# Layer scale, x + gamma * y: loads in one order on the SP queue, stores held back on the ACT queue, pieces of 40, 37, 40 and 11 rows

## The chip, the cores and the metric

The kernel runs on one core of a Trainium2 chip. The metric is the device time of one execution in microseconds (us). Beside it stands a profile of one execution, whose span runs from the first to the last instruction of the core. Engines are named as in the profile: PE is TensorE, DVE is VectorE, ACT is ScalarE, POOL is GpSimd, SP is SyncE; ACTq and SPq are the queues from which ACT and SP issue DMAs.

## The reference

```python
B, S, D = 1024, 16, 512          # x, y: [B, S, D] bfloat16, gamma: [D] bfloat16

def reference(x, y, gamma):
    return x + gamma * y
```

x, y and the output have 16.78 MB each, so 33.56 MB are read and 16.78 MB are written.

## The kernel before

The 16384 rows of 512 elements (1 KB each) are split over the 128 partitions, so that each partition owns 128 consecutive rows, 128 KB of each tensor. The kernel cuts these 128 rows into four pieces of 32 (`PIECE`, line 5). Every DMA moves one piece of one tensor: 4 MB, as 128 packets of 32 KB, one for each partition. The 16 DMA engines serve eight partitions each.

All of y has room on the core (`y_sb`, 128 KB per partition), and the result is written over it. x has two buffers of 32 rows (`xs`, line 46), so the third piece of x can be loaded only when the first has been added, and the fourth when the second has.

At the start a small DMA brings gamma, PE copies it to all partitions by a matrix product with a row of ones, and DVE writes that to `gamma_sb`. Then DVE works through the pieces in order (lines 95 to 113): it waits for y's piece, multiplies it by gamma in place (line 98), waits for x's piece, and adds x (line 104).

The order of the transfers is written out by hand, for two queues:

- ACT issues gamma, then the four loads of y one behind the other, then waits for the second piece's add and stores piece 1, waits for the fourth add and stores piece 3 (lines 86 to 93).
- SP issues x pieces 0 and 1, waits for the first add, issues x piece 2, waits for the second add, issues x piece 3 and the store of piece 0, waits for the third add and stores piece 2 (lines 75 to 83).

So loads of x and y run side by side on two queues, and stores begin behind loads on both. The first loads are moved to the front of the program (lines 118 to 124). `_take` (line 9) waits for a semaphore and subtracts what it waited for. SP waits at the end for both queues' stores (lines 115 and 116).

Of the kernel before, what the change touches and what calls it, by code (L numbers as in the profile page):

```python
# [3 lines left out]

PIECE = 32
MULT, ADD = mybir.AluOpType.mult, mybir.AluOpType.add


def _take(sem, n, eng):


    return eng.wait_ge(sem, n).then_inc(sem, -n)  # L12


def kernel(
    tc: tile.TileContext,
    x: bass.AP,
    y: bass.AP,
    gamma: bass.AP,
    out: bass.AP,  # L20
):

    nc = tc.nc
    P = nc.NUM_PARTITIONS
    tc.close()
    tc.compile()  # L29

    xf = x.flatten_outer_dims()
    yf = y.flatten_outer_dims()
    of = out.flatten_outer_dims()
    N, D = xf.shape
    rows = N // P
    n = rows // PIECE
    dt = xf.dtype
    xv = xf.rearrange("(p n) d -> p n d", p=P)
    yv = yf.rearrange("(p n) d -> p n d", p=P)
    ov = of.rearrange("(p n) d -> p n d", p=P)  # L40

    gamma_row = nc.alloc_sbuf_tensor("gamma_row", [1, D], dt).ap()
    ones_row = nc.alloc_sbuf_tensor("ones_row", [1, P], dt).ap()
    gamma_sb = nc.alloc_sbuf_tensor("gamma_sb", [P, D], dt).ap()
    y_sb = nc.alloc_sbuf_tensor("y_sb", [P, rows, D], dt).ap()
    xs = [nc.alloc_sbuf_tensor(f"x{i}", [P, PIECE, D], dt).ap() for i in range(2)]
    gamma_ps = nc.alloc_psum_tensor("gamma_ps", [P, D], mybir.dt.float32).ap()

    sem = nc.alloc_semaphore
    s_gamma, s_ones, s_ps, s_dve = sem("s_gamma"), sem("s_ones"), sem("s_ps"), sem("s_dve")  # L50
    s_x = [sem(f"s_x{c}") for c in range(n)]
    s_y = [sem(f"s_y{c}") for c in range(n)]
    s_sp, s_act = sem("s_sp"), sem("s_act")
    s_out_sp, s_out_act = sem("s_out_sp"), sem("s_out_act")

    def piece(c):
        return slice(c * PIECE, (c + 1) * PIECE)

    first = []

    def load(eng, dst, src, s):
        return eng.dma_start(out=dst, in_=src).then_inc(s, 16)


    first.append(load(nc.scalar, gamma_row, gamma.unsqueeze(0), s_gamma))
    nc.vector.memset(ones_row, 1.0).then_inc(s_ones, 1)  # L66
    _take(s_ones, 1, nc.tensor)
    _take(s_gamma, 16, nc.tensor)
    nc.tensor.matmul(gamma_ps, ones_row, gamma_row, start=True, stop=True).then_inc(s_ps, 1)  # L69
    _take(s_ps, 1, nc.vector)  # L70
    nc.vector.tensor_copy(out=gamma_sb, in_=gamma_ps).then_inc(s_dve, 1)  # L71
    _take(s_dve, 1, nc.vector)


    first.append(load(nc.sync, xs[0], xv[:, piece(0), :], s_x[0]))
    first.append(load(nc.sync, xs[1], xv[:, piece(1), :], s_x[1]))
    _take(s_sp, 1, nc.sync)
    load(nc.sync, xs[0], xv[:, piece(2), :], s_x[2])
    _take(s_sp, 1, nc.sync)
    load(nc.sync, xs[1], xv[:, piece(3), :], s_x[3])  # L80
    nc.sync.dma_start(out=ov[:, piece(0), :], in_=y_sb[:, piece(0), :]).then_inc(s_out_sp, 16)
    _take(s_sp, 1, nc.sync)
    nc.sync.dma_start(out=ov[:, piece(2), :], in_=y_sb[:, piece(2), :]).then_inc(s_out_sp, 16)


    for c in range(n):
        i = load(nc.scalar, y_sb[:, piece(c), :], yv[:, piece(c), :], s_y[c])
        if c < 2:
            first.append(i)
    _take(s_act, 1, nc.scalar)  # L90
    nc.scalar.dma_start(out=ov[:, piece(1), :], in_=y_sb[:, piece(1), :]).then_inc(s_out_act, 16)
    _take(s_act, 1, nc.scalar)
    nc.scalar.dma_start(out=ov[:, piece(3), :], in_=y_sb[:, piece(3), :]).then_inc(s_out_act, 16)

    for c in range(n):
        yt = y_sb[:, piece(c), :]
        _take(s_y[c], 16, nc.vector)
        nc.vector.tensor_tensor(  # L98
            out=yt, in0=yt, in1=gamma_sb[:, None, :].to_broadcast([P, PIECE, D]), op=MULT
        ).then_inc(s_dve, 1)  # L100
        _take(s_x[c], 16, nc.vector)
        _take(s_dve, 1, nc.vector)

        i = nc.vector.tensor_tensor(out=yt, in0=xs[c % 2], in1=yt, op=ADD)  # L104
        if c == 0:
            i.then_inc(s_sp, 1)
        elif c == 1:
            i.then_inc(s_dve, 1)
            _take(s_dve, 1, nc.vector)
            nc.vector.sem_inc(s_sp, 1)  # L110
            nc.vector.sem_inc(s_act, 1)
        else:
            i.then_inc(s_sp if c == 2 else s_act, 1)

    _take(s_out_sp, 32, nc.sync)
    _take(s_out_act, 32, nc.sync)

    main = nc.main_func.blocks[0].instructions
    names = {i.ins.name for i in first}
    for b in nc.main_func.blocks[1:]:  # L120
        for i in [i for i in b.instructions if i.name in names]:
            b.instructions.remove(i)
    for k, i in enumerate(first):
        main.insert(1 + k, i.ins)


# [1 line left out]
_INS = ['x', 'y', 'gamma']  # L128
_OUTS = [((1024, 16, 512), 'bfloat16')]


# [23 lines left out]
```

## Time and profile before

| what | value |
|---|---|
| time, median of 10 runs | 121.17 us (120.83 to 121.4) |
| the profiled execution's own time | 121.16 us |
| its span, first to last instruction | 119.8 us |
| DVE busy | 70.3 us (59%), four multiplies and four adds of 8.69 us |
| first multiply starts, last add starts | 24.38 us, 86.34 us |
| moved | 50.33 MB, mean 420 GB/s |
| the two DMA queues' packet time | 49.9% and 48.7% of 16 engines' span |

In the profile's slices each digit is the busy share of a fortieth of the span in tenths. A queue's share is the time of its packets divided by the time of 16 engines over the whole span. q1 is the SP queue, q10 the ACT queue. An operation of VectorE is told as output<-inputs, partitions x elements and type. "L104" is line 104 of the kernel; waits show line 12, the helper `_take`. The trace also holds a record for every DMA packet: its start, its duration, its size and its queue.

### The profile page before, as it was taken

What the parts mean: (1) busy time and instruction counts of PE and PEld (TensorE: products, weight loads), DVE (VectorE), ACT (ScalarE), POOL (GpSimd) and SP (SyncE); (2) the same over time, 40 slices, a digit from 0 to 9 for tenths busy, and PEclk for the clock granted to TensorE, in tenths of its full rate; (3) what the DMA queues carried; (4) which work ended last, traced back from release to release, by engine and by line L of the source; (5) the groups of instructions that cost most, each with busy time, mean ns of one, the idle gap of its engine ahead of it and who ended that gap; (6) DMA issues with size and microseconds to landing.
All of it is one profiled execution on the core that took longest, in us unless ns stands there. A gap on an engine that the chain in (4) does not pass through costs nothing. (4 is left out here: it accounts for less than half of the span.)

```text
span 119.8 us, 90 instructions
## 1 busy us (share of the span) xinstructions
PE 0.6 (0%) x1; PEld 0.1 (0%) x1; DVE 70.3 (59%) x10; POOL 0.2 (0%) x4
## 2 busy tenths in 40 slices
PE   0100000000000000000000000000000000000000
PEld 0000000000000000000000000000000000000000
DVE  0100000089999999999899999999999700000000
POOL 0000000000000000000000000000000000000000
DMA  8999998989898989999999999999999999999994
GB/s 252 448 394 481 394 481 372 503 350 525 350 514 361 503 372 481 394 470 405 427 448 394 481 394 394 394 394 470 405 459 416 448 427 438 427 427 448 405 459 197
DMA packets 1730, 50.33 MB, mean 420 GB/s; under 512 B 193, under 2 KB 194, under 8 KB 194
## 3 DMA queue, kind: packets, MB, share of 16 engines
q1 hardware_dynamic: 864, 25.17, 49.9%
q10 hardware_dynamic: 866, 25.17, 48.7%
HBM read 33.56 MB, written 16.78 MB: 420 GB/s over the span
## 5 line engine op out<-in xcount | busy, mean ns | idle before, releaser
L98 DVE TENSOR_TENSOR y_sb<-y_sb,gamma_sb 128x16384 bf16<-128x16384 bf16 x4 | 34.8, 8690 | 18.9 <-DVEq L12 18.9
L104 DVE TENSOR_TENSOR y_sb<-x,y_sb 128x16384 bf16<-128x16384 bf16 x4 | 34.8, 8692 | 0.6
L71 DVE CAST gamma_sb<-gamma_ps 128x512 bf16<-128x512 f32 x1 | 0.7, 692 | 2.6 <-DVEq L12 2.6
L66 DVE MEMSET ones_row<- 1x128 bf16 x1 | 0.2, 165 | 2.7 <-PEq L29 2.7
L69 PE MATMUL gamma_ps<-gamma_row,ones_row 1*128 1x512 bf16 x1 | 0.6, 581 | 4.7 <-PEq L12 4.7
L69 PEld LDWEIGHTS gamma_ps<-gamma_row,ones_row 1*128 1x128 bf16 x1 | 0.1, 98 | 4.7 <-issue 4.7
L139 POOL MEMSET const-bfloat16-1.0<- 128x1 bf16 x1 | 0.1, 101 | 0.0
L139 POOL MEMSET const-uint8-127<- 128x1 uint8 x1 | 0.1, 101 | 0.0
L139 POOL MEMSET const-float32-0.0<- 128x1 f32 x1 | 0.1, 98 | 0.2 <-issue 0.2
L139 POOL MEMSET const-float32-1.0<- 128x1 f32 x1 | 0.1, 98 | 0.0
## 6 DMA issues: line engine op xcount, KB each, us to landing
x<-in_x_dram SPq DMA_DIRECT2D x4, 4096.0 KB, 24.7
y_sb<-in_y_dram ACTq DMA_DIRECT2D x4, 4096.0 KB, 47.3
out_dram<-y_sb ACTq DMA_DIRECT2D x2, 4096.0 KB, 30.5
out_dram<-y_sb SPq DMA_DIRECT2D x2, 4096.0 KB, 41.9
gamma_row<-in_gamma_dram ACTq DMA_DIRECT2D x1, 1.0 KB
```

The lines of the kernel that those rows point to most:

```text
L66: nc.vector.memset(ones_row, 1.0).then_inc(s_ones, 1)
L69: nc.tensor.matmul(gamma_ps, ones_row, gamma_row, start=True, stop=True).then_inc(s_ps, 1)
L71: nc.vector.tensor_copy(out=gamma_sb, in_=gamma_ps).then_inc(s_dve, 1)
L98: nc.vector.tensor_tensor(out=yt, in0=yt, in1=gamma_sb[:, None, :].to_broadcast([P, PIECE, D]), op=MULT).then_inc(s_dve, 1)
L104: i = nc.vector.tensor_tensor(out=yt, in0=xs[c % 2], in1=yt, op=ADD)
L139: nc = _bacc.Bacc("TRN2", target_bir_lowering=False, num_devices=1)
```

## The change

Every load is issued by SP, in one list: x and y piece 0 (40 rows), x and y piece 1 (37 rows), all the rest of y (51 rows in one DMA), x piece 2 (40 rows), x piece 3 (11 rows). The x buffer is one tensor of 77 rows; x piece 2 takes the place of piece 0, so its load waits for the first add, and x piece 3 lies within the place of piece 1, so its load waits for the second. Gamma stays with ACT, which otherwise issues only the stores, now two of 64 rows each (64 KB per partition). The first store waits for `s_go`, which PE sends once the load of x rows 77 to 117 has landed, and for the first two adds; the second waits for all four adds. DVE learns of that landing from PE too (`s_rel`). Adds count up one semaphore (`s_add`), and both stores count up one (`s_out`), which SP reads at the end. On DVE the order of operations is the same, on pieces of the new sizes.

```diff
--- before.py
+++ after.py
@@ -2,7 +2,20 @@
 import concourse.tile as tile
 from concourse import mybir
 
-PIECE = 32
+PIECES = [40, 37, 40, 11]
+SP = [('x', 0, 40, 0), ('y', 0, 40), ('x', 40, 77, 40), ('y', 40, 77), ('y', 77, 128), ('x', 77, 117, 0), ('x', 117, 128, 40)]
+ACT = [('g',), ('s', 0, 64), ('s', 64, 128)]
+EARLY = (2, 1)
+RELEASE = ('x', 77, 117, 0)
+DVE = [('m', 0), ('a', 0), ('m', 1), ('a', 1), ('m', 2), ('a', 2), ('m', 3), ('a', 3)]
 MULT, ADD = mybir.AluOpType.mult, mybir.AluOpType.add
 
 
@@ -22,7 +35,6 @@
 
 
 
     nc = tc.nc
     P = nc.NUM_PARTITIONS
     tc.close()
@@ -33,7 +45,9 @@
     of = out.flatten_outer_dims()
     N, D = xf.shape
     rows = N // P
-    n = rows // PIECE
+    n = len(PIECES)
+    assert sum(PIECES) == rows
+    starts = [sum(PIECES[:c]) for c in range(n + 1)]
     dt = xf.dtype
     xv = xf.rearrange("(p n) d -> p n d", p=P)
     yv = yf.rearrange("(p n) d -> p n d", p=P)
@@ -43,26 +57,70 @@
     ones_row = nc.alloc_sbuf_tensor("ones_row", [1, P], dt).ap()
     gamma_sb = nc.alloc_sbuf_tensor("gamma_sb", [P, D], dt).ap()
     y_sb = nc.alloc_sbuf_tensor("y_sb", [P, rows, D], dt).ap()
-    xs = [nc.alloc_sbuf_tensor(f"x{i}", [P, PIECE, D], dt).ap() for i in range(2)]
+    x_loads = [w for w in SP + ACT if w[0] == "x"]
+    y_loads = [w for w in SP + ACT if w[0] == "y"]
+    stores = [w for w in SP + ACT if w[0] == "s"]
+    for loads in (x_loads, y_loads, stores):
+        assert sum(w[2] - w[1] for w in loads) == rows
+    x_rows = max(w[3] + w[2] - w[1] for w in x_loads)
+    x_sb = nc.alloc_sbuf_tensor("x_sb", [P, x_rows, D], dt).ap()
     gamma_ps = nc.alloc_psum_tensor("gamma_ps", [P, D], mybir.dt.float32).ap()
 
     sem = nc.alloc_semaphore
     s_gamma, s_ones, s_ps, s_dve = sem("s_gamma"), sem("s_ones"), sem("s_ps"), sem("s_dve")
-    s_x = [sem(f"s_x{c}") for c in range(n)]
-    s_y = [sem(f"s_y{c}") for c in range(n)]
-    s_sp, s_act = sem("s_sp"), sem("s_act")
-    s_out_sp, s_out_act = sem("s_out_sp"), sem("s_out_act")
-    def piece(c):
-        return slice(c * PIECE, (c + 1) * PIECE)
-    first = []
-    def load(eng, dst, src, s):
-        return eng.dma_start(out=dst, in_=src).then_inc(s, 16)
-    first.append(load(nc.scalar, gamma_row, gamma.unsqueeze(0), s_gamma))
+    s_load = {w: sem("s_" + "_".join(map(str, w[:2]))) for w in x_loads + y_loads}
+    s_add, s_go, s_rel, s_end, s_out = sem("s_add"), sem("s_go"), sem("s_rel"), sem("s_end"), sem("s_out")
+    added = [a for kind, *a in DVE if kind == "a"]
+    order = {a[0]: k for k, a in enumerate(added)}
+    def meets(a, b, c, d):
+        return a < d and c < b
+    def pieces_of(a, b):
+        return [c for c in range(n) if meets(starts[c], starts[c + 1], a, b)]
+    def x_at(row):
+        return next(w[3] + row - w[1] for w in x_loads if w[1] <= row < w[2])
+    def frees(w):
+        old = x_loads[: x_loads.index(w)]
+        old = [v for v in old if meets(v[3], v[3] + v[2] - v[1], w[3], w[3] + w[2] - w[1])]
+        return [c for v in old for c in pieces_of(v[1], v[2])]
+    early = []
+    def ring(eng, what, n_early):
+        known, went = 0, False
+        for k, w in enumerate(what):
+            kind = w[0]
+            need = frees(w) if kind == "x" else pieces_of(w[1], w[2]) + list(w[3:]) if kind == "s" else []
+            need = max((order[c] + 1 for c in need), default=0)
+            if kind == "s" and not went:
+                _take(s_go, 1, eng)
+                went = True
+            if need > known:
+                eng.wait_ge(s_add, need)
+                known = need
+            if kind == "g":
+                i = eng.dma_start(out=gamma_row, in_=gamma.unsqueeze(0)).then_inc(s_gamma, 16)
+            elif kind == "x":
+                to = x_sb[:, w[3] : w[3] + w[2] - w[1], :]
+                i = eng.dma_start(out=to, in_=xv[:, w[1] : w[2], :]).then_inc(s_load[w], 16)
+            elif kind == "y":
+                r = slice(w[1], w[2])
+                i = eng.dma_start(out=y_sb[:, r, :], in_=yv[:, r, :]).then_inc(s_load[w], 16)
+            else:
+                r = slice(w[1], w[2])
+                i = eng.dma_start(out=ov[:, r, :], in_=y_sb[:, r, :]).then_inc(s_out, 16)
+            if k < n_early:
+                early.append(i.ins)
+    ring(nc.sync, SP, EARLY[0])
+    ring(nc.scalar, ACT, EARLY[1])
     nc.vector.memset(ones_row, 1.0).then_inc(s_ones, 1)
     _take(s_ones, 1, nc.tensor)
     _take(s_gamma, 16, nc.tensor)
@@ -71,57 +129,51 @@
     nc.vector.tensor_copy(out=gamma_sb, in_=gamma_ps).then_inc(s_dve, 1)
     _take(s_dve, 1, nc.vector)
 
-    first.append(load(nc.sync, xs[0], xv[:, piece(0), :], s_x[0]))
-    first.append(load(nc.sync, xs[1], xv[:, piece(1), :], s_x[1]))
-    _take(s_sp, 1, nc.sync)
-    load(nc.sync, xs[0], xv[:, piece(2), :], s_x[2])
-    _take(s_sp, 1, nc.sync)
-    load(nc.sync, xs[1], xv[:, piece(3), :], s_x[3])
-    nc.sync.dma_start(out=ov[:, piece(0), :], in_=y_sb[:, piece(0), :]).then_inc(s_out_sp, 16)
-    _take(s_sp, 1, nc.sync)
-    nc.sync.dma_start(out=ov[:, piece(2), :], in_=y_sb[:, piece(2), :]).then_inc(s_out_sp, 16)
-    for c in range(n):
-        i = load(nc.scalar, y_sb[:, piece(c), :], yv[:, piece(c), :], s_y[c])
-        if c < 2:
-            first.append(i)
-    _take(s_act, 1, nc.scalar)
-    nc.scalar.dma_start(out=ov[:, piece(1), :], in_=y_sb[:, piece(1), :]).then_inc(s_out_act, 16)
-    _take(s_act, 1, nc.scalar)
-    nc.scalar.dma_start(out=ov[:, piece(3), :], in_=y_sb[:, piece(3), :]).then_inc(s_out_act, 16)
-    for c in range(n):
-        yt = y_sb[:, piece(c), :]
-        _take(s_y[c], 16, nc.vector)
-        nc.vector.tensor_tensor(
-            out=yt, in0=yt, in1=gamma_sb[:, None, :].to_broadcast([P, PIECE, D]), op=MULT
-        ).then_inc(s_dve, 1)
-        _take(s_x[c], 16, nc.vector)
-        _take(s_dve, 1, nc.vector)
-        i = nc.vector.tensor_tensor(out=yt, in0=xs[c % 2], in1=yt, op=ADD)
-        if c == 0:
-            i.then_inc(s_sp, 1)
-        elif c == 1:
-            i.then_inc(s_dve, 1)
-            _take(s_dve, 1, nc.vector)
-            nc.vector.sem_inc(s_sp, 1)
-            nc.vector.sem_inc(s_act, 1)
+    _take(s_load[RELEASE], 16, nc.tensor)
+    nc.tensor.sem_inc(s_go, 1)
+    nc.tensor.sem_inc(s_rel, 1)
+    landed, open_mults = set(), 0
+    def need(loads, c):
+        for w in loads:
+            if w not in landed and meets(starts[c], starts[c + 1], w[1], w[2]):
+                if w == RELEASE:
+                    _take(s_rel, 1, nc.vector)
+                else:
+                    _take(s_load[w], 16, nc.vector)
+                landed.add(w)
+    for kind, *args in DVE:
+        c = args[0]
+        yt = y_sb[:, starts[c] : starts[c + 1], :]
+        if kind == "m":
+            need(y_loads, c)
+            g = gamma_sb[:, None, :].to_broadcast([P, PIECES[c], D])
+            nc.vector.tensor_tensor(out=yt, in0=yt, in1=g, op=MULT).then_inc(s_dve, 1)
+            open_mults += 1
         else:
-            i.then_inc(s_sp if c == 2 else s_act, 1)
-    _take(s_out_sp, 32, nc.sync)
-    _take(s_out_act, 32, nc.sync)
+            need(x_loads, c)
+            if open_mults:
+                _take(s_dve, open_mults, nc.vector)
+                open_mults = 0
+            at = x_at(starts[c])
+            xt = x_sb[:, at : at + PIECES[c], :]
+            nc.vector.tensor_tensor(out=yt, in0=xt, in1=yt, op=ADD).then_inc(s_add, 1)
+    nc.scalar.sem_inc(s_end, 1)
+    _take(s_end, 1, nc.sync)
+    _take(s_add, n, nc.sync)
+    _take(s_out, 16 * len(stores), nc.sync)
 
     main = nc.main_func.blocks[0].instructions
-    names = {i.ins.name for i in first}
+    names = {i.name for i in early}
     for b in nc.main_func.blocks[1:]:
         for i in [i for i in b.instructions if i.name in names]:
             b.instructions.remove(i)
-    for k, i in enumerate(first):
-        main.insert(1 + k, i.ins)
+    for k, i in enumerate(early):
+        main.insert(1 + k, i)
 
 
 # ---- launch: one core; inputs and outputs as the reference has them ----
```

## The prediction

> **What bounds the kernel now.** I read the busy shares, then the slices, the queues, the stretches, and last the timeline around the final store.
>
> ```profile
> span 119.8 us, 90 instructions
> PE 0.6 (0%) x1; PEld 0.1 (0%) x1; DVE 70.3 (59%) x10; POOL 0.2 (0%) x4
> ...
> DMA  8999998989898989999999999999999999999994
> ...
> DMA packets 1730, 50.33 MB, mean 420 GB/s; under 512 B 193, under 2 KB 194, under 8 KB 194
> ...
> q1 hardware_dynamic: 864, 25.17, 49.9%
> q10 hardware_dynamic: 866, 25.17, 48.7%
> ```
>
> The only busy compute engine works 59% of the span; the two DMA queues together hold the 16 engines for 98.6% of it, 118.1 us. 1730 less 194 small packets leaves 1536 large ones, 96 per engine of 32 KB each (one partition's rows of one piece), so 1.23 us a packet. In the trace's packet records the usual packet takes 1.213 us. The mean is higher for four reasons, per engine: the first packets (start 1.00 to 1.36 us into the span, mean 1.858) lose 0.64; the next two 0.03; packets between 44 and 73 us average 1.216 and lose 0.08; and around 73 to 77 us, where the first store meets the last x load, two load packets lose 0.79. Sum for the slowest engine: 1.36 + 96 x 1.213 + 1.54 + 12 semaphore packets of 0.009 = 119.4 us, and the last packet does end at 119.39. Landing adds 0.33, the end of the program 0.11: 119.83. The execution lasts 121.16, so 1.36 lies around the span; the median of the runs is 121.17, so the two can be compared directly.
>
> The stretches show the same rate with loads only and with stores only, and the dip between (columns: stretch, length, busy time of PE, PEld, DVE, POOL, clock, DMA share, GB/s):
>
> ```profile
> 5.00:72.00 67.00, 0.26 (x1) 0.00 (x0) 47.43 (x7) 0.00 (x0) 1.00 1.00 432
> 72.00:78.00 6.00, 0.00 (x0) 0.00 (x0) 5.83 (x2) 0.00 (x0) 1.00 1.07 404
> 78.00:118.00 40.00, 0.00 (x0) 0.00 (x0) 16.89 (x2) 0.00 (x0) 1.00 1.00 433
> ```
>
> The last rows of the timeline (start, length):
>
> ```profile
> 86.34 8.69 DVE L104 TENSOR_TENSOR y_sb<-x,y_sb 128x16384 bf16<-128x16384 bf16 x1
> 95.14 0.35 ACTq L93 DMA_DIRECT2D out_dram<-y_sb  x1
> ```
>
> VectorE ends at 95.03, the last store is issued 0.11 later, and 24 us of stores are still to drain. So the engines' bytes set the end, and VectorE only through when it releases a store.
>
> **What the Trainium skill says.** "DMA: Bandwidth & Descriptors", section "Where 436 GB/s comes from", gives a ceiling of 435.2 GB/s; the 432 and 433 above are 99% of it. Same page, "Issuing engines are not separate DMA queues": DMAs of any issuer share the 16 engines. The trace agrees: from 36 to 45 us only the ACT ring has packets, across the boundary from the second to the third y load, and they still follow each other every 1.21 us. So one ring for loads costs nothing by itself. Same page, "Latency and other measured facts": first byte on this path after about 0.6 us, memory latency 0.2 us, 2 us at high load. Here the first load's packet came 1.0 us after issue on idle engines; what load adds is the slow rival below.
>
> **The change, part by part.** *Bytes*: unchanged, 3 x 128 rows of 1 KB on each of 128 partitions; a row on all partitions is 8 KB per engine, 8/32 x 1.213 = 0.303 us.
>
> *Fewer, larger packets*: seven loads and two stores make 8 x 9 = 72 packets per engine, not 96. An 8 KB instruction-fetch packet takes 0.3075 us; four are 1.230 against 1.213, so a packet has a fixed part of 0.017/3 = 0.006 us. 24 fewer: -0.14, -0.03 with three fewer semaphore packets. Bounds: 0 (if a 64 KB row is cut in two or the fixed part belongs to fetches only, near 0) to -0.25.
>
> *Two rings to one for the loads*: the 0.08 lost between 44 and 73 us is with two rings, 36 to 44 us on one ring shows none. I take -0.08, bounds -0.08 to +0.1.
>
> *First store*: the 0.79 loss cannot vanish by order alone; a stream must turn from loads to stores once. Nearest row: the first load, 0.64. I take that, -0.15; bounds -0.79 to +0.5.
>
> *Waits*: I lay out the new order for the slowest engine (start 1.36 + 0.67 = 2.03, then 0.303 a row, landing 0.33). y0 ends after 80 rows and lands at 26.6 (24.3 before). VectorE needs 8.69/32 = 0.272 us a row and operation, 0.15 from multiply to add, -0.08 from add to multiply, as before; eight operations and 69.5 us in all either way. Piece 0 ends at 48.6. y1 (154 rows) lands at 49.05, half a microsecond of idle. Piece 1 ends at 69.4, piece 2 at 91.1 (y2 and x2 landed long before), piece 3 at 97.2. SP's wait for add 0 stands before x2, its wait for add 1 before x3; queued behind these waits are only those two loads. SP passes the second at 69.4, while x2 runs until 76.3, so x3 is in the ring 7 us early. PE's wait for x2 stands behind the finished matmul and holds up nothing; VectorE takes its word at about 80, where it is three microseconds old. The stores are queued behind ACT's wait for it: x2 lands at 76.65, and four semaphore steps of 0.11 give an issue at 77.1. Cover until its first packet: x3, 11 rows, until 2.03 + 256 x 0.303 = 79.65, 2.5 us. The first store (64 rows, 19.4 us) then ends at 79.65 + 0.64 + 19.4 = 99.65. The second needs add 3, 97.2: issued at 97.3, 2.3 us ahead. With the 1.0 to 1.4 us of the first load both leads suffice. If the second's cover is gone, each microsecond of delay beyond it is a microsecond of time.
>
> *Rest*: SP's final waits and ACT's handover to it come before the last landing and cost nothing under it; shared counting of the stores is read only at its full value. Gamma's path still ends 20 us before the first multiply.
>
> Sum: 121.16 - 0.14 - 0.03 - 0.08 - 0.15 = 120.76.
>
> **Rivals.** *A, continuous transfers*, as summed: 120.8, by itself 120.5 to 121.1. *B, the turn to stores costs nothing*: then the first store ends at 99.0, and VectorE's chain takes over: issue 97.3, packets from 98.7 on the slowest engine, start-up 0.64 if the ring is nearly dry, 19.4 of data, 0.44 to the end, 1.36 around: 120.5. For it: after the turn 40 us of stores run at full rate; against it: the one start and the one turn in this trace both paid.
>
> *C, stores start late and leave the engines dry; slower.* Under load the trace shows long delays from issue to first packet: third x load 3.4 to 4.6 us (issue 42.0), last store 4.1 to 4.8 (95.14). If that is latency and not queueing, the store issued at 77.1 starts around 77.1 + 3.8 = 80.9, 1.2 us after the loads end; the second then finds its ring hardly dry, since the first is late too. 120.8 + 1.2 = 122.0. It decides once the delay exceeds the leads of 2.5 and 2.3 us. For it: the delays themselves. Against it: each is about 1.0 us plus the packet in service and one or two more of the other ring, which looks like packets already taken in, and gamma's packet, issued at 0.13 to 0.65, came at 2.95 behind one single packet of x.
>
> *D, nothing gained*: packets cost by bytes alone, and the turn costs 0.79 again or a dry spell of some tenths stands ahead of the second store: 121.1.
>
> **How the numbers follow.** A 0.42, B 0.18, C 0.22, D 0.18. A measurement of this kernel can tell about 0.2%, 0.24 us, from no change: faster is below 120.93. Most of A (0.37) and B (0.18) give faster 0.55; D and the slow side of A give same 0.22; C, 0.22, and the end of D slower 0.23. Forecast 120.8, that of A. The range from 120.4 to 121.9 takes in A, B, D and the milder part of C, and leaves out about 0.18. A and B alone: 120.4 to 121.1.
>
> **What would show it.** Right: loads at 432 GB/s on one queue without a gap until 79 to 80 us; the first store issued at about 77.1; the last add ending at about 97.2 and the last store issued at once; no DMA slice under 9 at 79 or 99 us; span 119.4. The turn shows as slow packets at 79. C would show as a dip there or ahead of the second store; B as an end 21 to 22 us after VectorE's last add. Wrong altogether: load packets above 1.213 us per 32 KB, stores of 64 KB rows slower per byte, or an add ending after 99.

## The result, and the profile after

The changed kernel takes 120.00 us (median of 8 runs, 119.92 to 120.06), the kernel before 121.23 in the runs beside it: a ratio of 0.9898, 95% interval 0.9888 to 0.9909. That is 1.2 us gained where 0.4 was forecast, and 0.4 us below the low end of the range, 120.4.

The page of the changed kernel, first the shares and slices, then the queues:

```profile
span 118.8 us, 84 instructions
...
PE 0.6 (0%) x1; PEld 0.1 (0%) x1; DVE 70.2 (59%) x10; POOL 0.2 (0%) x4
...
DMA  7999999999999999979696999998899889988891
...
DMA packets 1299, 50.33 MB, mean 424 GB/s; under 512 B 146, under 2 KB 147, under 8 KB 147
...
q1 hardware_dynamic: 1008, 33.55, 66.0%
q10 hardware_dynamic: 290, 16.78, 32.6%
```

VectorE is as busy as before. The loads are 66.0% of the engines' span on SP's queue and the stores 32.6% on ACT's: 98.6% together, the same as before, of a span 1.0 us shorter. 1299 less 147 small packets leaves 1152 large ones, 72 per engine. The single digits of 6 and 7 in the middle of the slice row (50 to 65 us), and the 8s from 80 us on, are no dry spells: this view books a packet where it starts, and the packets are now long against a slice of 2.97 us (1.93 us for 51 rows, 2.42 for 64). In the packet records each engine's packets follow one another there without a pause. The stretches show the same distortion when they are short (stretch, length, busy times, clock, DMA share, GB/s):

```profile
75.00:79.00 4.00, 0.00 (x0) 0.00 (x0) 4.00 (x1) 0.00 (x0) 1.00 0.82 344
79.00:82.00 3.00, 0.00 (x0) 0.00 (x0) 2.85 (x2) 0.00 (x0) 1.00 1.62 700
```

344 and then 700 GB/s is a row of 64 KB store packets that all begin just after 79 us, not a pause and a burst. Where a fraction of a microsecond matters, the packet records have to be read instead, as below.

The timeline around the two stores (start, length; the ACTq row merges both stores, from the first issue to the end of the second):

```profile
69.41 10.82 DVE L153 TENSOR_TENSOR y_sb<-y_sb,gamma_sb 128x20480 bf16<-128x20480 bf16 x1
77.06 20.75 ACTq L116 DMA_DIRECT2D out_dram<-y_sb  x2
...
94.35 3.09 DVE L162 TENSOR_TENSOR y_sb<-x_sb,y_sb 128x5632 bf16<-128x5632 bf16 x1
```

The first store is issued at 77.06 and the last add ends at 97.44, against 77.1 and 97.2 in the forecast: the schedule came out as laid out. What differs is in the packets. I compare each packet with the usual (median) packet of its size (11 KB 0.422 us, 32 KB 1.213, 64 KB 2.418), and call what is over that the excess. It is summed over all packets and divided by the 16 engines. The turn is the time in which loads end and stores begin, 72 to 78 us before and 76 to 80 after.

| | before | after |
|---|---|---|
| all packets at their usual time | 116.45 | 116.24 |
| excess of the first packets | 0.64 | 0.66 |
| excess at the turn from loads to stores | 0.79 | 0.04 |
| other excess | 0.11 | 0.10 |
| last packet ends, us in the span | 119.39 | 118.33 |

So 0.75 of the 1.06 us by which the last packet ends earlier is the turn, and 0.21 is the fewer packets. Before, every engine has one to three load packets at the turn that take up to 2.3 us instead of 1.213. After, no packet there is more than 0.1 us over its usual time. The store packets that follow are not shorter than usual in either kernel, so the time is lost and not only moved. The experiments ask why.

### The profile page after: what moved, and what is told of

Same layout as the page of the kernel before. It is cut to its first block, busy times and chain, and to the rows that moved or that the text cites. A ratio compares the mean times of both kernels' runs of the same rounds, so it can differ in the third digit from the quotient of the medians.

```text
span 118.8 us, 84 instructions
## 1 busy us (share of the span) xinstructions
PE 0.6 (0%) x1; PEld 0.1 (0%) x1; DVE 70.2 (59%) x10; POOL 0.2 (0%) x4
## 2 busy tenths in 40 slices
DMA packets 1299, 50.33 MB, mean 424 GB/s; under 512 B 146, under 2 KB 147, under 8 KB 147
## 3 DMA queue, kind: packets, MB, share of 16 engines
q10 hardware_dynamic: 290, 16.78, 32.6%
## 5 line engine op out<-in xcount | busy, mean ns | idle before, releaser
L153 DVE TENSOR_TENSOR y_sb<-y_sb,gamma_sb 128x20480 bf16<-128x20480 bf16 (+2 forms) x4 | 34.8, 8688 | 20.7 <-DVEq L25 20.7
L162 DVE TENSOR_TENSOR y_sb<-x_sb,y_sb 128x20480 bf16<-128x20480 bf16 (+2 forms) x4 | 34.8, 8692 | 0.6
```

The source lines that it names most:

```text
L153: nc.vector.tensor_tensor(out=yt, in0=yt, in1=g, op=MULT).then_inc(s_dve, 1)
L162: nc.vector.tensor_tensor(out=yt, in0=xt, in1=yt, op=ADD).then_inc(s_add, 1)
```

## The experiments

The expectations name theories of what makes load packets slow at the turn:

- T1: the turn costs something only while load packets of the other queue are still to come.
- T2: it costs something only if a store is queued behind a load on its own queue.
- T3: it always costs the same, or the slow packets don't come from the turn at all.
- T4, after the first four runs: it costs whenever stores are known to the engines while loads are still to be served.
- T5, also after these: it depends on the queue that the stores use.

**The kernel before with its first ACT store held.** The idea was to move only the start of the store.

```diff
+    _take(s_y[3], 16, nc.tensor)
+    nc.tensor.sem_inc(s_go, 1)
+    nc.tensor.sem_inc(s_rel, 1)
...
+    _take(s_go, 1, nc.scalar)
     _take(s_act, 1, nc.scalar)
     nc.scalar.dma_start(out=ov[:, piece(1), :], in_=y_sb[:, piece(1), :]).then_inc(s_out_act, 16)
```

> Kernel before, with one edit: the first store of the ACT queue (piece 1) is issued only once the last y load has landed, so that its packets reach the engines when the x load on the other queue is nearly through. Theory T1 (a turn from loads to stores costs 0.8 us only while load packets of the other queue are still being served; after them it is free): the slow packets of 73 to 77 us are gone, 121.2 - 0.7 = 120.5 us, x piece 3 landing at about 80 instead of 85. T2 (the cost comes from a store queued behind a load on its own queue): the first store is no longer queued, also about 120.5. T3 (the slow stretch is not tied to the turn, or is a cost that any turn pays): 121.2, and the stretch is still there, at the new turn or at 73 us.

Measured 121.12 us, ratio 0.9994 (0.9982 to 1.0006): no gain. x landed at 80.1 to 80.6 as expected, but slow load packets stood at 77 us, 0.44 us per engine. Two stores could be the cause: SP's store of piece 0, which was still queued behind x piece 3 and which the expectation of T2 overlooked, and ACT's own, issued at 76.78 while packets of x were running until 80.2. So this run decides neither T1 nor T2.

**The first store on SP, unheld.**

```diff
-SP = [..., ('x', 117, 128, 40)]
-ACT = [('g',), ('s', 0, 64), ('s', 64, 128)]
+SP = [..., ('x', 117, 128, 40), ('s', 0, 64)]
+ACT = [('g',), ('s', 64, 128)]
```

> Changed kernel, with the first store moved from the ACT queue to the end of the SP queue, right behind the last x load, with no hold on it but the two adds. T1 (only mixing costs): loads and stores still follow each other, no slow packets, 120.0 us. T2 (a store queued behind a load costs): 0.6 to 0.8 us of slow packets at 79 us, about 120.7. T3: 120.0.

Measured 121.70 us, ratio to before 1.0035 (1.0023 to 1.0047), 1.7 us above the changed kernel. The store is issued at 69.77:

```profile
69.77 0.44 SPq L116 DMA_DIRECT2D out_dram<-y_sb  x1
```

The load packets of 77 to 80 us carry 0.83 us of excess although no store packet runs before 79.9: a store waiting behind them is enough. Loads and store share one queue here, so T1 is out. A second cost, not expected: the last store, first on the ACT queue when SP's runs out, begins with 0.79 us of excess per engine at 99 us.

**32-row pieces, early and late release.** Two kernels that differ only in how x piece 3 is loaded, and in which part releases the stores:

```diff
-SP = [..., ('x', 64, 96, 0), ('x', 96, 128, 32)]
-RELEASE = ('x', 64, 96, 0)
+SP = [..., ('x', 64, 96, 0), ('x', 96, 117, 32), ('x', 117, 128, 53)]
+RELEASE = ('x', 96, 117, 32)
```

> Changed kernel with four pieces of 32 rows and four stores of 32 rows, the stores released when x piece 2 has landed: 32 rows of x piece 3 are still to be loaded when the first store comes, so the two are mixed for some 15 us. T1: the slow packets are back at about 71 to 75 us, 0.8 us; with 16 more packets per engine (0.1) 120.9 us. T2: no store is queued behind a load, no slow packets, 120.1. T3: 120.1. The last add would end at about 96, some 13 us ahead of need, so no dry spell under any.

> As the kernel with four pieces of 32 rows, but x piece 3 is loaded as 21 and 11 rows, and the stores are released when the 21 rows have landed: only 11 rows are left when the first store comes, as in the changed kernel. T1: no slow packets, 0.8 us less than with the early release, 120.1 us. T2 and T3: same as with the early release, within 0.1.

Measured 121.09 us (early; ratio 0.9995, 0.9985 to 1.0005) and 120.13 us (late; 0.9912, 0.9892 to 0.9931). The rows of the stores in the timeline, merged from the first issue on, early release and then late:

```profile
70.73 26.79 ACTq L116 DMA_DIRECT2D out_dram<-y_sb  x4
```

```profile
77.24 19.88 ACTq L116 DMA_DIRECT2D out_dram<-y_sb  x4
```

The slow packets are in the first, 0.8 us of excess at 72 to 75, and at the turn of the second at most 0.01. The view of one stretch, early release and then late:

```profile
66.00:90.00 24.00, 0.00 (x0) 0.00 (x0) 22.34 (x4) 0.00 (x0) 1.00 1.02 425
```

```profile
66.00:90.00 24.00, 0.00 (x0) 0.00 (x0) 22.69 (x4) 0.00 (x0) 1.00 1.02 433
```

The two rates, 425 and 433 GB/s, differ in the right direction, but this view is too coarse to carry the reading: the run with the first ACT store held shows 433 in the same stretch although its loads lost 0.44 us. The packet records and the times decide. T2 is out as well: in the early kernel no store stood behind a load on its queue. T3 is out, because the late kernel turns from loads to stores without the cost. One load queue, one order and one store queue bring nothing that these runs can tell by themselves (121.09); the late release brings the microsecond.

**Both stores of the kernel before held**, until 21 of x piece 3's 32 rows have landed:

```diff
-    load(nc.sync, xs[1], xv[:, piece(3), :], s_x[3])
+    load(nc.sync, xs[1][:, :21, :], xv[:, 96:117, :], s_x[3])
+    load(nc.sync, xs[1][:, 21:, :], xv[:, 117:128, :], s_x3b)
+    _take(s_go_sp, 1, nc.sync)
...
+    _take(s_go, 1, nc.scalar)
     _take(s_act, 1, nc.scalar)
...
+    _take(s_x[3], 16, nc.tensor)
+    nc.tensor.sem_inc(s_go, 1)
+    nc.tensor.sem_inc(s_go_sp, 1)
+    nc.tensor.sem_inc(s_rel, 1)
```

> Kernel before (two queues, 32-row pieces), with x piece 3 loaded as 21 and 11 rows, and the first store of each queue issued only once the 21 rows have landed, as the changed kernel does it. T4 (stores pay 0.7 to 1.0 us when they are known to the engines, queued behind loads or on the other queue, while load packets are still to be served; they pay nothing when they come in about the last microsecond of the loads): no slow packets, 121.2 - 0.8 = 120.4 us. T5 (it matters which queue the stores use: behind loads on their own queue they pay): the SP queue still carries loads and then its store, slow packets stay, about 121.1.

Measured 120.38 us, ratio 0.9921 (0.9904 to 0.9937), excess at the turn at most 0.01. Two load queues, two store queues and 32-row pieces stay; the hold, with the cut of x piece 3 that it needs, takes 0.9 of the 1.2 us. (The cut alone doesn't do it: the runs with other cuts further down have it and pay.) The larger packets account for most of the rest: this run has 104 packets per engine, 0.27 us more at their usual time than the 72 of the changed kernel. The same stretch, of the kernel before and of this one:

```profile
66.00:90.00 24.00, 0.00 (x0) 0.00 (x0) 23.53 (x4) 0.00 (x0) 1.00 1.00 419
```

```profile
66.00:90.00 24.00, 0.00 (x0) 0.00 (x0) 23.70 (x4) 0.00 (x0) 1.00 1.00 427
```

Again the direction is right, 8 of 427 GB/s, and the packet records decide.

**Stores on the loads' own queue, but held.** In the run with the first store on SP the take of `s_go` is moved to SP; in the other both stores are in SP's list.

```diff
-            if kind == "s" and not went and eng is nc.scalar:
+            if kind == "s" and not went and eng is nc.sync:
```

> As the run with the first store on the SP queue behind the last x load (121.7 us, 0.83 us of slow load packets at 76 to 80 us and 0.79 us on the second store's first packets at 98 us), but that store is now held until x piece 2 has landed, as in the changed kernel. T4: the slow load packets at 76 to 80 us are gone, about 120.9. T5: they stay, 121.7. The second store, alone on the ACT queue, starts 0.79 us slow under both if that cost belongs to the change of queue.

```diff
+SP = [..., ('x', 117, 128, 40), ('s', 0, 64), ('s', 64, 128)]
+ACT = [('g',)]
```

> As the changed kernel, but both stores on the SP queue as well, the first held until x piece 2 has landed; ACT issues gamma alone. T4: no slow packets at either turn, 120.0 us. T5: 0.8 us of slow load packets at 76 to 80, 120.8. In both the second store follows the first on its queue and starts at full rate.

Measured 120.82 us and 120.05 us; excess at the turn 0.04 and 0.03. T5 is out and T4 stands: with the hold, the queue doesn't matter for the turn. The 0.7 us on the last store, which opens the ACT queue at 98 us, is there in the first (0.72) and absent in the second, which makes the 0.8 us between the two.

**Held to the very end.**

```diff
-RELEASE = ('x', 77, 117, 0)
+RELEASE = ('x', 117, 128, 40)
```

> Changed kernel, with the stores held until the last x load (11 rows) has landed instead of the one before. The engines run dry: landing at about 80.1, issue at 80.5, first packet at 81.5 to 82 instead of 79.4, so 120.0 + 2.3 = 122.3 us if a store starts at full rate on idle engines (T4), 123.0 if the start-up that the prediction gave the second store, 0.64, exists when the engines are dry.

Measured 121.94 us, ratio 1.0049 (1.0031 to 1.0068). The timeline has the first issue at 80.46:

```profile
80.46 17.37 ACTq L116 DMA_DIRECT2D out_dram<-y_sb  x2
```

The packets start at 81.33 to 81.48, 0.9 to 1.0 us later, where the changed kernel's start at 79.14 to 79.64, and their excess is 0.04. So idle engines started a store at full rate here: no start-up like the 0.66 us of the first load. The 1.9 us lost against the changed kernel are the pause alone.

**How late is late enough.** The 32-row kernel with the late release, cut as 16 and 16 and as 11 and 21 rows:

```diff
-('x', 96, 117, 32), ('x', 117, 128, 53)
+('x', 96, 112, 32), ('x', 112, 128, 48)
```

> As the kernel of 32-row pieces with a late release (x piece 3 as 21 and 11 rows, 120.13 us), but cut as 16 and 16: 16 rows, 4.9 us, are still to be loaded when the release comes, some 3.2 us when the stores reach the engines (release to first packet takes about 1.65 us). T4 as a step (full cost whenever stores arrive more than about 1.5 us before the loads end): slow load packets of 0.7 to 0.9 us, 120.9 us. T4 graded (cost in step with the loads left): 0.2 to 0.4 us, 120.4.

> The same with 11 and 21 rows: 21 rows left at the release, 4.7 us when the stores reach the engines. T4 as a step: 120.9 us as with 16. T4 graded: 0.4 to 0.6 us, 120.7.

The rows of the stores, cut as 16 and 16 and then as 11 and 21:

```profile
75.61 21.48 ACTq L116 DMA_DIRECT2D out_dram<-y_sb  x4
```

```profile
74.17 23.02 ACTq L116 DMA_DIRECT2D out_dram<-y_sb  x4
```

Measured 120.92 us and 121.03 us, excess 0.60 and 0.93, against 120.13 and 0.01 with 11 rows left. As an estimate, a store reaches the engines 0.9 to 1.0 us after its issue, as it did on idle engines. Then some 3 us of loads are left in the first of the two and some 4.4 in the second, against 1.0 to 1.8 in the runs that paid 0.04 or less. The cost is nearer to the step than to the graded forecast, but three points don't give its shape: 0.60 is not the full price.

The traces show one thing more. In all six traces that paid at the turn (the kernel before among them), the first load packet that is over 0.1 us late there starts 2.8 to 3.3 us before the first store packet, however long ago that store had been issued: 17 us in the kernel before, 10 in the run with the first store on SP, 4 to 5 in the 32-row kernels. In the changed kernel only 2.1 to 2.6 us lie between the issue of the first store and its packets.

**The last add later**, by a second copy of gamma on VectorE ahead of it:

```diff
+            if c == 3:
+                nc.vector.tensor_copy(out=gamma_sb, in_=gamma_ps)
             at = x_at(starts[c])
```

> Changed kernel with a second copy of gamma from PSUM (0.69 us) ahead of the last add, so that the last store is issued at about 98.1 instead of 97.44 and reaches the engines at 99.0 (0.9 us from issue to first packet on idle engines). The first store ends at 98.5 to 98.9. If VectorE's chain and the transfers now meet, as the trace of the changed kernel suggests: 120.0 + 0.4 to 0.7 = 120.4 to 120.7 us. If there is half a microsecond of slack left: 120.0 to 120.2.

Measured 120.07 us. The last store's row of the timeline, in the changed kernel and in this one:

```profile
97.47 0.34 ACTq L116 DMA_DIRECT2D out_dram<-y_sb  x1
```

```profile
97.95 0.34 ACTq L116 DMA_DIRECT2D out_dram<-y_sb  x1
```

Half a microsecond later, and the last packet ends at 118.34 instead of 118.33. The second store's packets now start at 98.80 to 98.95 on all engines, where they had started at 98.47 to 98.96: 15 of the 16 engines now wait for it, up to half a microsecond, where two had waited in the changed kernel. The end hardly moves because the engines that end the first store early had time to spare, and the last start is the same to 0.01 us. So about half a microsecond of slack was there, and the forecast that the two now meet missed it; with nearly all engines waiting, a still later add should cost time, which was not tried.

**Loads on two queues, the changed kernel's pieces.**

```diff
+SP = [('x', 0, 40, 0), ('x', 40, 77, 40), ('x', 77, 117, 0), ('x', 117, 128, 40)]
+ACT = [('g',), ('y', 0, 40), ('y', 40, 77), ('y', 77, 128), ('s', 0, 64), ('s', 64, 128)]
+EARLY = (2, 2)
```

> Changed kernel with its loads split over both queues: x on SP, y (in the same pieces) on ACT ahead of the stores, which are held as before. Here the stores are issued after the y loads of their queue are all through, and late. T4: no slow packets at the turn; the two queues cost the 0.08 us that the kernel before showed between 44 and 73 us: 120.1 us. If one queue for the loads is worth more than that, the time shows it.

Measured 122.46 us, ratio 1.0092 (1.0071 to 1.0113), a miss by 2.4 us. The turn is clean (0.01). But y piece 0 shares the engines with x and lands at 27.6 to 29.3 us instead of 26.2 to 26.7, and all of VectorE moves with it. First multiply (in brackets its wait for y) and last store of this run:

```profile
29.40 10.82 DVE L153 TENSOR_TENSOR y_sb<-y_sb,gamma_sb 128x20480 bf16<-128x20480 bf16 x1 [22.62 <-DVEq L25]
...
100.30 0.35 ACTq L116 DMA_DIRECT2D out_dram<-y_sb  x1
```

The first store has drained by 98.5 to 99.0, the second's packets begin at 101.2: dry for 2.2 to 2.8 us, and in the row of this run there is a slice of 3 us in which no packet starts:

```profile
GB/s 216 433 433 433 433 433 433 433 442 488 488 400 400 400 400 521 431 535 234 492 492 398 371 433 433 406 547 563 346 346 476 563 0 346 346 693 346 346 346 346
```

So the other part of the design, one order on one queue, brought nothing measurable with 32-row pieces, but the pieces of 40 rows with two 64-row stores need it: they leave VectorE half a microsecond of slack.

## Why the prediction was right or wrong

**What bounds the kernel**: right. The engines' packets set the end before and after, at 98.6% of both spans, and half a microsecond on VectorE's chain moved nothing. Little slack is left there, though.

**Bytes, larger packets**: right, within its bounds. 24 packets fewer cost 0.21 us less at the usual times (0.14 forecast). One packet of 64 KB takes 2.418 us and two of 32 KB take 2.426, so a packet's fixed part is nearer to 8 ns than to the 6 that the fetch packets gave, and a 64 KB row is not cut in two.

**Two rings to one, -0.08** (a ring is a queue): not seen. The other excess went from 0.11 to 0.10, and it varies from about 0.06 to 0.5 between the runs, so a term of this size can't be told. It happens to cancel what the packets brought beyond their forecast.

**Waits and schedule**: right within 0.3 us: first multiply 26.85 for 26.6, first store 77.06 for 77.1, last add 97.44 for 97.2, loads through at 79.1 to 79.6 for 79.65.

**First store, -0.15**: this is the step that failed. It gave the turn a price of 0.64 for the nearest row, the first load, and said that the loss cannot vanish by order alone. It all but vanished by order alone: 0.79 to 0.04, so the term was -0.75 and not -0.15. The loss had been read as the price of turning. The runs show that it is paid when stores stand ready, on either queue, while load packets are still to come, and not when the same stores are held back until the loads are nearly through. The kernel before had both its first stores queued long before, some 17 us ahead of the first store packet:

```profile
59.71 0.35 ACTq L91 DMA_DIRECT2D out_dram<-y_sb  x1
...
59.98 0.42 SPq L81 DMA_DIRECT2D out_dram<-y_sb  x1
```

The change issues the first store at 77.06, so that by the estimate above it reaches the engines 1.1 to 1.7 us before the loads end. The bound was stated (-0.79), but was given only the chance of rival B.

**Rival B's floor of 120.5** failed too, and with it the low end of the range. It took 0.64 for a store's start-up on an almost dry ring and the slowest engine's 1.36 us from issue to packet, both from the first load. A store on idle engines starts after 0.9 to 1.0 us and loses 0.04. With these, and the last store issued at 97.47, VectorE's chain alone allows about 119.7, and A's sum with the turn at -0.75 is 120.2. Of the 0.2 left, 0.1 is the ends of the engines lying closer together (the last packets of the 16 end within 0.80 us before and within 0.55 after); the rest, the profiled execution against the median (120.08 and 120.00).

**Rival C** did not come: the first store found all engines busy, and only two engines waited for the second, at most 0.2 us. The store issued at 77.06 had packets running 2.1 to 2.6 us later, as soon as the loads were through. This fits the prediction's reading that the delays of 3.4 to 4.8 us under load are packets already taken in, but no run tested that. The Trainium skill, "DMA: Bandwidth & Descriptors", section "Issuing engines are not separate DMA queues", says that DMAs run on the same 16 engines whoever issues them. It held in its main point: loads and stores on one queue took 120.05 us, loads on one and stores on the other 120.00. But a last store that alone opened the other queue paid 0.7 to 0.8 us in two runs, so where a DMA is issued was not always without cost.

**Sums of the prediction**: some are off by a few hundredths, and nothing hangs on them. The sum for the slowest engine gives 119.46 and not 119.4, 121.16 less 119.83 is 1.33 and not 1.36, and the first store's end adds up to 99.7 and not 99.65.

**Open**: what the engine does when it slows the loads. A view of the engines' insides isn't in the trace. Shown are the condition (stores ready while some 3 us of loads or more remain; free at 1.0 to 1.8 us by the estimate above, with the limit somewhere between), the size (0.4 to 0.9 us per engine, once), and that neither the mixing of load and store packets, nor the queue, nor one packet size is needed for it: load packets of 11, 16, 21 and 32 KB all showed it. It is not any new DMA that does this: from 5 to 72 us one load follows another in the kernel before, and its packets lose 0.1 us in all. What makes a store that opens the ACT queue behind SP's stores pay 0.7 to 0.8 was not tried further; a store that opened it on idle engines, and the changed kernel's first store, which opens it behind SP's loads, paid no more than 0.04.

## What to carry to other kernels

Where the DMA engines are busy from end to end, look at single packets around each turn from loads to stores: a fraction of a microsecond per engine can hide where the slices show full digits. Try holding the first store back until a last small load is all that is left, large enough to cover the way from release to first packet, and no larger. Here 1.4 MB (11 rows, 3.3 us) was right; nothing left cost 1.9 us, and 16 rows instead of 11, in the 32-row kernel, cost 0.8. Don't price a turn or a start by another kind of transfer: the first load's start-up didn't carry over to stores.

## What the runs showed of the hardware

Stores that were queued or issued while some 3 us of loads or more were still to be served slowed those loads by 0.4 to 0.9 us per engine, once, even on the same queue and before any store packet ran; the slow packets began 2.8 to 3.3 us ahead of the first store packet. Stores that reached the engines in about the last 1.0 to 1.8 us of the loads (estimated from the issue) cost 0.00 to 0.04. A store on idle engines began 0.9 to 1.0 us after its issue at full rate, while the first load lost 0.5 to 0.7 on its first packet. A store that opened the ACT queue just as stores on SP's ran out lost 0.72 and 0.79 us in two runs. A packet of 64 KB took 2.418 us, two of 32 KB 2.426.
